# Two attention and two FFN blocks on one core: GpSimd constants ahead of the first layer-norm powers, and the second attention layer's last output chunk as seven block products

## The chip, the cores and the metric

The kernel runs on one core of one Trainium2 chip. The metric is the device time of one launch in microseconds (us); the time given is the median of three launches.

## The reference

Four residual blocks in a row, with the same weights used twice. S is 2048 tokens, D is 512, there are 32 heads of 16, the hidden width of the FFN is 1376; inputs, weights and output are bf16.

```python
def _A_ref(x, wqkv, wo):          # linear attention, 32 heads of 16
    q, k, v = ...                 # x @ wqkv
    phi = lambda t: jnp.where(t > 0, t + 1, jnp.exp(t)) + 1e-6
    pq, pk = phi(q), phi(k)
    kv = jnp.einsum("bhsd,bhse->bhde", pk, v)
    z = jnp.einsum("bhsd->bhd", pk)
    num = jnp.einsum("bhqd,bhde->bhqe", pq, kv)
    den = jnp.einsum("bhqd,bhd->bhq", pq, z)[..., None] + 1e-6
    return ... num / den ... @ wo

def _B_ref(x, w1, w2):
    return jnp.maximum(x @ w1, 0) @ w2

x = A_x
x = x + _A_ref(_layernorm(x), A_wqkv, A_wo)
x = x + _B_ref(_layernorm(x), B_w1, B_w2)
x = x + _A_ref(_layernorm(x), A_wqkv, A_wo)
x = x + _B_ref(_layernorm(x), B_w1, B_w2)
```

## The kernel before

The tokens lie in 16 tiles of 128, and four tiles make a chunk. The four blocks are layers 0 to 3: 0 and 2 are attention, 1 and 3 the FFN. The residual `xres` (128 x 512 a tile, f32) and all weights stay in SBUF.

**How the order is made.** The Python code doesn't issue instructions as it is read. Each operation is added to a graph with its engine, what it reads and writes, and a duration (the constants `C_...` in ns). A list scheduler (L383) then builds one queue for each engine: of the operations whose inputs it holds for ready it takes the one with the smallest `prio`, which is its place in the code plus an entry of the table `HINTS` (L340). An entry `"name!"` picks the engine where the code allows two. Operations of DVE and GpSimd that must not stand side by side carry a lock; names that begin with an entry of `SMALLS` (L58) have the short kind. An `odep` between two operations sets their order in a queue only; it is no wait on the chip.

**A layer norm in the first layer.** `ln_stats_first` (L772) takes BN_STATS (L773) and BN_AGGR (L774) of a tile on DVE. `ln_part_first` (L776) makes `rstd`: for the tiles named in `RSTD_ACT` by two small ScalarE instructions, Ln and Exp (L779 and L781); otherwise by a small add on DVE (`veps`, L784) and a power on GpSimd (L786). Tiles 0 to 5 are done one by one, 6 and 7 together, 8 to 11 together, 12 to 15 together. `ln_norm` (L808) then normalises with one instruction a tile into `xn` (L811), and the transposed copy `Tb` is made: for tiles 0 to 5 by TensorE and a copy out of PSUM (L847), for the others by DMA transposes that SP issues (`tr_dma`, L826). When a chunk has been transposed, `ones_col` (L1042) has GpSimd set the last column of its `xn` to 1.0, so that the products with phi(K) also give the sum z; the matmuls that read `big` (phi of K) and `xn` wait for this.

**Constants.** GpSimd fills the constants at the start (L694 to L760): the identity (L697), masks for the heads by affine selects (`m1f` L751, `bmask` L753, `hm` L757 and L760), and two memsets (L748, L749).

**Attention.** phi(K) and phi(Q) are in the unit store `big`; the sums over tokens give K/V products, which are folded with `wo` into `Mf` (128 x 4 x 512). For each chunk `a_fin_chunk` (L1182) then multiplies phi(Q) by `Mf`: four tiles with four matmuls of 512 columns each, and for each tile `resid` (L886) adds the product to the residual on DVE (L889), which also gives the row sum, and `sq` (L894) squares it on ScalarE for the row's variance. `ln_half` makes the next layer's norm for two tiles at a time. q and k products of some chunks (`a7`), the FFN's first products (`b_h7`) and its second (`b_out`) are seven block products in place of eight, with sums of blocks on DVE (for q and k, L951 and its neighbours), drains on DVE such as L1558 and a copy of one product into another PSUM bank on ScalarE (`seed`, L624). `f7` (L1207) and `f7_sums` (L1198) do the same for the output products of attention; the table `F7` (L573), which says for which layers and chunks, has none. All matmuls of these groups are issued in `mm_group` (L878, matmul L882).

**Loads.** SP issues all loads but one of `wqkv`, the DMA transposes, and the spread transfers of the attention denominators (L1155, four groups of four a layer). The first FFN weight is loaded at L726, the second at L727 and L730.

The step that picks between the two forms of the output products:

```python
def p2(t):                       # L1734, once for each chunk
    if t in F7[layer]:
        f7(t, first_layer)
    else:
        a_fin_chunk(t, first_layer)
    if t == 0 and F7[layer]:
        f7_sums()
```

## Time and profile before

| | us |
|---|---|
| median of 3 launches | 263.32 (263.13 to 263.42) |
| the profiled launch | 263.28 |
| its span in the trace | 261.5 |
| granted TensorE clock, mean | 1.0 of full speed |

"Span" is the stretch from the first to the last recorded instruction. PE is TensorE's matmuls, PEld its weight loads, DVE VectorE, ACT ScalarE, POOL GpSimd, SP the engine that issues DMAs; a letter q behind an engine is its own queue. The costliest GpSimd rows of the page's groups (line, engine, operation, output and inputs, shapes, number | busy us, mean ns of one | idle time before and what ended it):

```profile
L803 POOL TENSOR_TENSOR rstd<-veps,nhalf 128x2 f32<-128x2 f32 x24 | 17.9, 747 | 13.7 <-DVE veps L801 13.1
L816 POOL TENSOR_SCALAR xn<-xres,mean,rstd 128x512 f16<-128x512 f32 x12 | 10.1, 839 | 0.3
L795 POOL TENSOR_SCALAR mean<-s 128x2 f32<-128x2 f32 x24 | 8.6, 361 | 51.1 <-DVE xres L889 49.9
```

The first two are the power and the normalisation of the later layer norms, the third the row means. GpSimd is idle for most of the span; its idle time, like that of any engine that isn't the bound, costs nothing by itself.

### The profile page before, as it was taken

The page shows a single profiled execution, that of the slowest core. Times are in us where ns is not written, and L with a number is a line of the kernel's source. Part 1 is how long each engine was busy: PE and PEld are TensorE (multiplying, and loading weights), DVE is VectorE, ACT ScalarE, POOL GpSimd, SP SyncE. Part 2 cuts the span into 40 slices and gives each one's busy share as a digit, 9 for nine tenths or more (in the row PEclk, how much of TensorE's full clock was granted, in tenths as well). Part 3 has the DMA queues.
Part 4 walks back from the last instruction along what each step waited for, and adds up shares of the span by engine and source line. Part 5 has one row for each costly group of instructions (what it writes and reads, how often), then busy time and mean ns, then how long its engine had stood idle before and what let it go on. Part 6 is the DMA issues. An engine that isn't in the chain of part 4 may idle for free.

```text
span 261.5 us, 5847 instructions
## 1 busy us (share of the span) xinstructions
PE 255.0 (98%) x2166; PEld 199.2 (76%) x2176; DVE 231.7 (89%) x572; ACT 194.9 (75%) x426; POOL 68.9 (26%) x159
## 2 busy tenths in 40 slices
PE   7999799999999999999999999999999999999995
PEld 3654378744788888888988878774478889988884
DVE  5999979699999998899999989859988987996874
ACT  4899979769999569598999899885999746441200
POOL 1144900009834025012530440002863500000000
PEclk9999999999999999999999999999999999999999
DMA  6758860635644004400524031048351154210104
GB/s 200 282 136 150 305 213 0 153 90 120 96 64 94 10 20 83 80 4 0 101 42 43 1 59 25 3 102 192 71 106 36 36 69 120 43 40 3 80 3 160
DMA packets 46268, 22.46 MB, mean 86 GB/s; under 512 B 35904, under 2 KB 44704, under 8 KB 46240
## 3 DMA queue, kind: packets, MB, share of 16 engines
q1 hardware_dynamic: 45968, 21.83, 36.1%
q8 instruction: 17, 0.28, 0.5%
q10 hardware_dynamic: 272, 0.26, 0.4%
q14 instruction: 11, 0.09, 0.1%
HBM read 7.14 MB, written 2.10 MB: 35 GB/s over the span
## 4 chain that ended last, share of the span: by engine, by line
PE 87%; DVE 4%; issue 3%; ACT 3%; DMA 2%; POOL 1%
PE ps L882 86%; DVE bst L773 2%; DMA Tb<-xn 1%; DVE xn L811 1%; DMA xin<-in_A_x_dram 1%; POOL hm L757 1%; ACT escr L864 1%; ACT xres L864 1%; ACT big L862 1%; ACT Tb L847 0%; PE ps L841 0%; PE ps L768 0%; DVE mv L774 0%; ACT rstd L781 0%; DVE KVT L1088 0%
## 5 line engine op out<-in xcount | busy, mean ns | idle before, releaser
L882 PE MATMUL ps<-big,xn 128*128 128x256 bf16 (+1 forms) x220 | 31.8, 286 | 1.9 <-POOL xn L1043 1.7
L624 ACT ACTIVATE ps<-ps 128x512 f32<-128x512 f32 (+1 forms) x41 | 22.1, 547 | 15.3 <-PE ps L882 14.3
L882 PE MATMUL ps<-w,big 128*128 128x256 bf16 (+1 forms) x256 | 32.5, 272 | 0.0
L897 ACT ACTIVATE sqscr<-xres 128x512 bf16<-128x512 f32 x48 | 29.9, 624 | 3.3 <-DVE xres L889 2.5
L882 PE MATMUL ps<-Mf,big 128*128 128x512 bf16 x126 | 28.5, 379 | 0.1
L882 PEld LDWEIGHTS ps<-big,xn 128*128 128x128 f16 x224 | 21.2, 98 | 8.5 <-POOL xn L1043 2.0
L882 PEld LDWEIGHTS ps<-w,big 128*128 128x128 bf16 (+1 forms) x256 | 25.0, 98 | 3.0
L1354 ACT ACTIVATE big<-ps 128x512 bf16<-128x512 f32 (+1 forms) x32 | 16.1, 514 | 12.1 <-PE ps L882 11.9
L1367 DVE CUSTOM_DVE_ANT_0 big<-ps,escr 128x512 bf16<-128x512 f32 (+1 forms) x38 | 22.7, 602 | 2.4 <-PE ps L882 1.9
L882 PE MATMUL ps<-Tb,w 128*128 128x256 f16 x160 | 24.0, 273 | 0.0
L882 PE MATMUL ps<-xn,w 128*128 128x256 f16 x160 | 23.7, 272 | 0.0
L1390 ACT ACTIVATE escr<-ps 128x512 f32<-128x512 f32 (+1 forms) x38 | 19.2, 536 | 5.6 <-PE ps L882 5.6
L882 PEld LDWEIGHTS ps<-Mf,big 128*128 128x128 bf16 x128 | 12.2, 98 | 14.5 <-ACT Mf L1095 0.5
L882 PE MATMUL ps<-xn,xin 128*128 128x256 f16 x160 | 23.0, 272 | 0.0
L795 POOL TENSOR_SCALAR mean<-s 128x2 f32<-128x2 f32 x24 | 8.6, 361 | 51.1 <-DVE xres L889 49.9
L803 POOL TENSOR_TENSOR rstd<-veps,nhalf 128x2 f32<-128x2 f32 x24 | 17.9, 747 | 13.7 <-DVE veps L801 13.1
L882 PE MATMUL ps<-wqkv,Tb 128*128 128x512 bf16 (+1 forms) x94 | 19.7, 343 | 0.1
L821 ACT ACTIVATE xn<-xres,nbias,rstd 128x512 f16<-128x512 f32 x24 | 18.8, 807 | 0.5 <-DVE nbias L805 0.3
L882 PE MATMUL ps<-w,Tb 128*128 128x96 bf16 (+2 forms) x176 | 17.3, 224 | 0.0
L882 PEld LDWEIGHTS ps<-Tb,w 128*128 128x128 bf16 x160 | 15.5, 98 | 2.2 <-DVE w L1314 0.2
L882 PEld LDWEIGHTS ps<-xn,xin 128*128 128x128 bf16 x160 | 15.6, 98 | 1.9
L882 PEld LDWEIGHTS ps<-xn,w 128*128 128x128 bf16 x160 | 15.4, 98 | 1.9
(145 smaller groups left out, 624.8 us busy)
## 6 DMA issues: line engine op xcount, KB each, us to landing
big<-rdc SPq DMA_DIRECT2D x32, 128.0 KB, 2.7
w<-in_B_w_dram SPq DMA_DIRECT2D x1, 1376.0 KB, 8.3
w<-in_B_w_dram SPq DMA_DIRECT2D x1, 1280.0 KB, 11.2
xin<-in_A_x_dram SPq DMA_DIRECT2D x2, 512.0 KB, 6.7
wqkv<-in_A_wqkv_dram SPq DMA_DIRECT2D x3, 256.0 KB, 5.1
xin<-in_A_x_dram SPq DMA_DIRECT2D x4, 128.0 KB, 2.9
xin<-in_A_x_dram SPq DMA_DIRECT2D x2, 256.0 KB, 5.1
wqkv<-in_A_wqkv_dram SPq DMA_DIRECT2D x1, 512.0 KB, 4.2
```

The costliest lines, as they stand in the source:

```text
L624: g.add(ACT, lambda e: e.activation(psv[:, b, 0:w], psv[:, src, 0:w], ACTF.Identity), [("ps", src)], [("ps", b)], C_ACT_PSUM if w == 512 e ...
L757: g.add(POOL, lambda e: e.affine_select(hm1[:].rearrange("p (a b) -> p a b", b=4), ones_v, [[-16, 8], [0, 4]], ALU.is_ge, 0.0, base=0, cha ...
L773: g.add(DVE, lambda e: e.bn_stats(bst[:, i, :], xin[:, i, :]), [("xin", i)] + list(after), [("bst", i)], C_DVE_BNST, name="bnst%d" % i)
L795: g.add(POOL, lambda e: e.tensor_scalar(mean[:, sl], s1[:, sl], -INV_D, None, ALU.mult), [("s1", i) for i in tl], [("mean", i) for i in tl ...
L803: g.add(POOL, lambda e: e.tensor_tensor(rstd[:, sl], veps[:, sl], nhalf[:, 0:n], ALU.pow), [("veps", lo), ("nhalf",)], [("rstd", i) for i ...
L821: (ACT, lambda e: e.activation(xn[:, i, :], src, ACTF.Identity, scale=rstd[:, i:i + 1], bias=nbias[:, i:i + 1]), C_ACT_SB_AP)],
L864: g.add(ACT, lambda e: e.activation(sap, psv[:, b, :], ACTF.Exp), [("ps", b)], skeys, C_ACT_EXP, name=name + "_exp")]
L882: last = e.matmul(o, l, r, start=st, stop=sp, skip_group_check=skip)
L897: g.add(ACT, lambda e: e.activation(sqscr[:, q, :], xres[:, i, :], ACTF.Square, scale=math.sqrt(INV_D), accum_out=s2[:, i:i + 1]), xr(i), ...
L1354: g.add_flex([(ACT, lambda e: e.activation(ap, src(), ACTF.Relu), C_ACT_PSUM if w == 512 else 270.0), (DVE, lambda e: e.tensor_scalar(ap, ...
L1367: g.add(DVE, lambda e: e._custom_dve(dve_ops.TENSOR_ADD_SAT, out=ap, in0=sh(psv[:, bank, 0:w]), in1=sh(other()), s0=FMAX, s1=0.0), [("ps", ...
L1390: g.add(ACT, lambda e, w=w: e.activation(q[:, 0:w], psv[:, bank, 0:w], ACTF.Identity), [("ps", bank)], key, C_ACT_PSUM if len(cs) == 2 els ...
```

## The change

- **Output products.** `F7` names chunk 3 of layer 2. Its 16 matmuls of 512 columns become 28 of 256 (seven products of four matmuls) by `f7`. `f7_sums` makes four sums of blocks of `Mf` on DVE, into the store `GT`; `f7` makes four sums of blocks of phi(Q), and drains the seven products into the residual by halves of the columns. The row sums then come as two halves, which GpSimd adds.
- **Constants first.** Every first-layer power that runs on GpSimd and every ones-column memset gets an order behind all GpSimd constants (`pool_setup`).
- **rstd.** `RSTD_ACT` loses 6, 8 and 12: the rstd of tiles 6 and 7, 8 to 11 and 12 to 15 is made by the add on DVE and a power on GpSimd of 128x2, 128x4 and 128x4.
- **DVE only.** The normalisations of tiles 6 and up in the first layer and the four subtractions `wvless` may no longer be taken by GpSimd.
- **Planner.** Two durations are raised (`C_POOL_POW`, `C_POOL_SMALL`), the memset of the ones column counts 90 ns, the small adds ahead of the first-layer powers (but tiles 4 and 5) get the name `fveps`, which is in `SMALLS`. The whole table `HINTS` is new: of some 1,800 entries 1,533 have another number.

```diff
-C_POOL_POW = 690.0
+C_POOL_POW = 720.0
...
-C_POOL_SMALL = 180.0
+C_POOL_SMALL = 230.0
...
-SMALLS = ("var", "veps", "nbias")
+SMALLS = ("var", "veps", "fveps", "nbias")
...
-HINTS = {"0.aqsum1": -54, "0.aqsum2": -52, "0.aqsum3": 52, "0.aqsum4": 70, "0.as1": 46, ...
+HINTS = {"0.aqsum1": -44, "0.aqsum2": -19, "0.aqsum3": -22, "0.aqsum4": 55, "0.as1": -13, ...
...
-        F7 = {0: (), 2: ()}
+        F7 = {0: (), 2: (3,)}
...
-        RSTD_ACT = (0, 1, 2, 3, 6, 8, 12)
+        RSTD_ACT = (0, 1, 2, 3)
...
+        pool_setup = [o for o in g.ops if o.eng == POOL]
...
-                  ..., C_DVE_SMALL, name="veps%d" % lo)
+                  ..., C_DVE_SMALL, name=("veps%d" if lo in (4, 5) else "fveps%d") % lo)
             g.add(POOL, lambda e: e.tensor_tensor(rstd[:, lo:hi], veps[:, lo:hi], nhalf[:, 0:hi - lo], ALU.pow),
-                  ..., C_POOL_POW1, name="rstd%d" % lo)
+                  ..., C_POOL_POW1, name="rstd%d" % lo).odeps.extend(pool_setup)
...
-                g.add_flex([(DVE, f, C_DVE_NORM_BF)] + ([(POOL, f, C_POOL_NORM)] if i >= PE_TILES else []),
+                g.add_flex([(DVE, f, C_DVE_NORM_BF)],
...
-                g.add_flex([(DVE, f, 335.0), (POOL, f, C_POOL_ADD)], ..., name="wvless%d" % m)
+                g.add_flex([(DVE, f, 335.0)], ..., name="wvless%d" % m)
...
-                  ..., C_POOL_SMALL / 2, name="onec%d" % lo)
+                  ..., 90.0, name="onec%d" % lo).odeps.extend(pool_setup)
```

The functions that now run for layer 2's last chunk, cut to their core (`t` is 3; a11 to a22 are blocks of phi(Q), b11 to b22 of `Mf`, `tw` the sums in `GT`, `sb_` the sums of phi(Q)):

```python
def f7_sums():
    ...
    for (o, a, b, rd, k) in ((t1, b12, b11, lo, 0), (t2, b22, t1, hi + gk[0], 1),
                             (t3, b22, b12, lo + hi, 2), (t4, b21, t2, hi + gk[1], 3)):
        g.add(DVE, ... e.tensor_tensor(o, a, b, ALU.subtract), ..., name="fwsum%d" % (k + 1))

def f7(t, first_layer):
    ...                                     # four sums of phi(Q) on DVE, fsum1 to fsum4
    BA, BC = alloc_bank(), alloc_bank()
    def prod(n, bank, X, W, opens, reads):  # 4 matmuls of 256 columns
    def mid(n, bank, i0, hf):               # DVE: two tiles' half columns += bank
    def fin(n, bank, i0, hf):               # DVE: the same tile by tile, with the row sum
    prod(1, BA, a11, b11, ...)
    BB = seed(BA, 512, ...)                 # ScalarE: copy of the bank
    prod(5, BC, sb_[0], tw[0], ...)
    prod(6, BA, sb_[1], tw[1], ...)
    mid("m5", BC, f1, 1)
    prod(2, BB, a12, b21, ...)
    mid("m6", BA, f0, 1)
    fin("c11", BB, f0, 0)
    prod(7, BA, sb_[2], tw[2], ...)
    prod(3, BC, sb_[3], b22, ...)
    fin("c22", BA, f1, 1)
    fin("c12", BC, f0, 1)
    sq(f0)
    sq(f0 + 1)
    ln_half(t, 0, halves=True)
    prod(4, BA, a22, tw[3], ...)
    ...
```

What the new table and the new orders do to the queues, at the three places that the prediction speaks of. In each row: line (in the changed kernel the lines from `pool_setup` on are 2 higher), operation, output and inputs, shape, and how many stand in a row.

GpSimd's queue from the identity on, up to the ones columns (`hm`, `m1f`, `bmask` are masks, `nbexp` and `hr` constants; `MEMSET xn` sets ones columns), before:

```order
L697 AFFINE_SELECT ident<-onesf 128x128
L786 TENSOR_TENSOR rstd<-veps,nhalf 128x1
L751 AFFINE_SELECT m1f<-onesf 128x128
L786 TENSOR_TENSOR rstd<-veps,nhalf 128x1
L811 TENSOR_SCALAR xn<-xin,mv,rstd 128x512
L1043 MEMSET xn 128x4 x2
L757 AFFINE_SELECT hm<-onesf 128x32
L1043 MEMSET xn 128x4
L753 AFFINE_SELECT bmask<-m1f 128x128
L748 MEMSET nbexp 128x2
L1043 MEMSET xn 128x4
L760 AFFINE_SELECT hm<-hm 128x32
```

The same place in the changed kernel:

```order
L697 AFFINE_SELECT ident<-onesf 128x128
L751 AFFINE_SELECT m1f<-onesf 128x128
L748 MEMSET nbexp 128x2
L757 AFFINE_SELECT hm<-onesf 128x32
L749 MEMSET hr 128x1024
L753 AFFINE_SELECT bmask<-m1f 128x128
L760 AFFINE_SELECT hm<-hm 128x32
L788 TENSOR_TENSOR rstd<-veps,nhalf 128x1
L788 TENSOR_TENSOR rstd<-veps,nhalf 128x2
L788 TENSOR_TENSOR rstd<-veps,nhalf 128x1
L788 TENSOR_TENSOR rstd<-veps,nhalf 128x4 x2
L1045 MEMSET xn 128x4 x4
```

All constants now stand behind the identity and ahead of the first power, three powers are new, the normalisation has gone to DVE, and the four memsets have only powers ahead of them; before, the select of L757 stood between the second and the third memset.

DVE's queue in the first layer, from the normalisations of chunk 2 to those of chunk 3 (`bst` and `mv` are the statistics; `Mf` takes the sums of the q weights here, since its place is still free; `escr` is the exp part of phi), before:

```order
L811 TENSOR_SCALAR xn<-xin,mv,rstd 128x512 x2
L773 BN_STATS bst<-xin 128x6 x3
L774 BN_AGGR mv<-bst 128x2
L811 TENSOR_SCALAR xn<-xin,mv,rstd 128x512
L774 BN_AGGR mv<-bst 128x2 x3
L935 TENSOR_TENSOR Mf<-wqkv 128x512
L935 TENSOR_TENSOR Mf<-wqkv,Mf 128x512
L870 TENSOR_SCALAR escr<-escr 128x1024
L811 TENSOR_SCALAR xn<-xin,mv,rstd 128x512 x3
```

The same place in the changed kernel:

```order
L813 TENSOR_SCALAR xn<-xin,mv,rstd 128x512 x3
L775 BN_STATS bst<-xin 128x6
L813 TENSOR_SCALAR xn<-xin,mv,rstd 128x512
L776 BN_AGGR mv<-bst 128x2
L775 BN_STATS bst<-xin 128x6 x2
L776 BN_AGGR mv<-bst 128x2 x3
L872 TENSOR_SCALAR escr<-escr 128x1024
L786 TENSOR_SCALAR veps<-mv 128x4
L937 TENSOR_TENSOR Mf<-wqkv 128x512
L813 TENSOR_SCALAR xn<-xin,mv,rstd 128x512 x3
```

There is one normalisation more (the one that GpSimd had), the small add `veps` stands ahead of the last three, one of the two weight sums has moved behind them, and the last three wait for a power on GpSimd.

PE's queue at layer 2's output products (`Mf` with `big`: output products; `GT` with `big`: those of the seven that read a sum of `Mf`; `Tb` with `w` and `xn` with `xin`: block products of layer 3, whose sums are kept in `xn` and `xin`), before:

```order
L882 MATMUL ps<-Mf,big 128x512 x4
L882 MATMUL ps<-wo,KVT 128x512 x2
L882 MATMUL ps<-Mf,big 128x512 x60
L882 MATMUL ps<-Tb,w 128x256 x8
L882 MATMUL ps<-w,Tb 128x96 x16
L882 MATMUL ps<-xn,xin 128x256 x8
```

The same place in the changed kernel:

```order
L884 MATMUL ps<-Mf,big 128x512 x34
L884 MATMUL ps<-Mf,big 128x256 x4
L884 MATMUL ps<-Mf,big 128x512 x12
L884 MATMUL ps<-GT,big 128x256 x4
L884 MATMUL ps<-Mf,big 128x256 x4
L884 MATMUL ps<-GT,big 128x256 x4
L884 MATMUL ps<-Tb,w 128x256 x8
L884 MATMUL ps<-GT,big 128x256 x4
L884 MATMUL ps<-Tb,w 128x256 x8
L884 MATMUL ps<-w,Tb 128x96 x16
L884 MATMUL ps<-Mf,big 128x256 x4
L884 MATMUL ps<-xn,xin 128x256 x18
```

The first of the seven products stands among the other chunks' wide matmuls, the rest among the first products of layer 3; a seventh, of `GT`, follows behind the last row. On SP the load of `w` at L727 has moved from ahead of the 16 spread transfers of layer 0 to behind 12 of them, and the load of `wvl` (L721) from behind five DMA transposes to behind three.

More of the change, by code (lines that the diff above doesn't have):

```diff
@@ L1039, in wv_less_last @@
                 f = (lambda e, m=m: e.tensor_tensor(wqkv[:, m, 2 * D:3 * D], wqkv[:, m, 2 * D:3 * D], wvl[:], ALU.subtract))
-                g.add_flex([(DVE, f, 335.0), (POOL, f, C_POOL_ADD)], [("wv0",), ("wvl",)], [("wv", m)], name="wvless%d" % m)
+                g.add_flex([(DVE, f, 335.0)], [("wv0",), ("wvl",)], [("wv", m)], name="wvless%d" % m)
         def ones_col(lo, n):
             g.add(POOL, lambda e: e.memset(xn[:, lo:lo + n, D - 1:D], 1.0),
-                  [], [("xn", i) for i in range(lo, lo + n)], C_POOL_SMALL / 2, name="onec%d" % lo)
+                  [], [("xn", i) for i in range(lo, lo + n)], 90.0, name="onec%d" % lo).odeps.extend(pool_setup)
         def a_zc():
```

6 lines of the change are left out of this document (3 added, 3 removed), and 438 rows, old and new, of the table HINTS.

## The prediction

> **What bounds the kernel now.** I read the page first: the share of each engine and the granted clock.
>
> ```profile
> span 261.5 us, 5847 instructions
> PE 255.0 (98%) x2166; PEld 199.2 (76%) x2176; DVE 231.7 (89%) x572; ACT 194.9 (75%) x426; POOL 68.9 (26%) x159
> PEclk9999999999999999999999999999999999999999
> ```
>
> PE is busy for 98% of the span at full clock, so time can come only from fewer TensorE columns or from PE's idle time. Where that idle time is, the chain of work that ended last says (start, length, what):
>
> ```profile
> 6.94 0.60 ACT Tb L847
> ...
> 7.66 0.21 ACT rstd L781
> ...
> 20.16 3.04 DMA Tb<-xn
> ...
> 23.25 0.23 POOL xn L1043
> 23.48 1.99 POOL hm L757
> 25.47 6.47 issue
> 31.94 0.12 POOL xn L1043
> ...
> 32.11 5.18 PE ps L882 x39
> ...
> 183.23 75.65 PE ps L882 x693
> ```
>
> From 32.11 to 258.88 the chain is PE alone but for 0.05 us at a time and one 0.43 us DVE step. Before 32.11 it runs through GpSimd. PE's own waits, the third view, have one entry over a microsecond behind the start:
>
> ```profile
> PE ps L882 <- POOL xn L1043: 1.7, 1, 1.7
> ```
>
> GpSimd's and PE's timelines show the place (start, length, engine, line; in brackets the idle time before):
>
> ```profile
> 23.30 8.69 POOL L757 TENSOR_SCALAR_AFFINE_SELECT hm<-onesf 128x32 f32<-128x32 f32 x1
> ...
> 32.84 0.27 POOL L760 TENSOR_SCALAR_AFFINE_SELECT hm<-hm 128x32 bf16<-128x32 f32 x1
> ...
> 29.81 0.60 PE L882 MATMUL ps<-big,xn 128*128 128x256 bf16 x4
> 32.11 1.15 PE L882 MATMUL ps<-big,xn 128*128 128x512 bf16 x5 [1.71 <-POOL xn L1043]
> ```
>
> The 128x32 affine select at L757 took 8.69 us, its sister at L760 0.27. Behind it stood the memset that writes the ones column, and for that PE waited. The four matmuls from 29.81 take 4 x 0.109 us (below), so the next group could have started at 30.24 and started at 32.11: **1.87 us lost**.
>
> **The change part by part.**
>
> *GpSimd constants first.* The select and the other constants move ahead of the first rstd, to where DVE runs its statistics. Seven short instructions stand behind the identity (ends at 1.39); even at 0.95 us each, the longest unhindered one shown (the 128x1024 memset), they end at 8.0. Before, the first power started only at 9.77, so they cost nothing.
>
> ```profile
> 9.77 0.56 POOL L786 TENSOR_TENSOR rstd<-veps,nhalf 128x1 f32<-128x1 f32 x1 [8.38 <-DVE veps L784]
> 63.20 0.95 POOL L749 MEMSET hr<- 128x1024 bf16 x1
> ```
>
> Then the ones-column memsets (0.12 and 0.23 us in the chain) have only powers ahead of them and their own waits for transposes. One of them stands behind the wait for the last chunk's transposes: normalised by 23.3 (below), issued and landed some 3.04 us later, with one more transpose ahead in SP's queue, they are there by 28; PE reads that memset's column 40 wide and 8 narrow matmuls behind its group at 21.84, at 21.84 + 8.63 + 0.87 = 31.3. The stall goes: **-1.87 us**. Next late would be DVE's phi of K, which the same products read; it comes next.
>
> *Rstd by power.* Six small ScalarE instructions (0.21) go and two copies out of PSUM come to it from DVE (0.60, as L847): nothing on balance. DVE gains three small adds, GpSimd one 128x2 and two 128x4 powers. No 128x4 power is in the trace. Nearest rows:
>
> ```profile
> L803 POOL TENSOR_TENSOR rstd<-veps,nhalf x24: 688/712/1007, 59.9 to 205.8; 128x2 f32<-128x2 f32 x24
> L786 POOL TENSOR_TENSOR rstd<-veps,nhalf x2: 552/556/560, 9.8 to 12.9; 128x1 f32<-128x1 f32 x2
> ```
>
> One column more costs 0.156 us, so four columns take an estimated 0.556 + 3 x 0.156 = 1.02 us. The low end is one column's 0.556. As a high end, an 8.69 us hold like the select's needs DVE to keep issuing; here DVE has one two-input sum queued (0.42, as L951 below) and then itself waits for the power, so 1.02 + 0.42 = 1.44. I take 1.02. Behind it on DVE stand the normalisation of tiles 12 to 15, then min-adds and the first sum for chunk 2's q products (L951):
>
> ```profile
> 20.06 0.30 DVE L774 BATCH_NORM_AGGREGATE mv<-bst 128x2 f32<-128x6 f32 x3
> 21.05 0.42 DVE L870 TENSOR_SCALAR escr<-escr 128x1024 bf16<-128x1024 bf16 x1
> 21.38 1.05 DVE L811 TENSOR_SCALAR xn<-xin,mv,rstd 128x512 f16<-128x512 bf16 x3
> 24.61 0.42 DVE L951 TENSOR_TENSOR big<-Tb 128x512 f16<-128x512 f16 x1
> 35.18 0.43 DVE L872 TENSOR_TENSOR big<-big,escr 128x512 bf16<-128x512 bf16 x1 [0.99 <-ACT big L862]
> ...
> 21.84 6.41 PE L882 MATMUL ps<-wqkv,Tb 128*128 128x512 bf16 x28
> ```
>
> Ahead of the last aggregates DVE gains tile 9's normalisation and a power wait and loses two copies out of PSUM, so I keep their 20.06. Spaced as here: aggregates and min-add 0.22 + 0.33, add 0.08, power 1.02 with some 0.15 of hand-over, so tile 12's normalisation starts at 21.9 (before: 21.38). Three normalisations (1.05), three min-adds (1.0), one normalisation (0.32) and two weight sums (0.7) later, at 25.0, comes the sum, done at 25.4. PE has the same columns ahead of its group at 21.84 in both orders; in the new one 16 wide and 4 narrow matmuls follow (0.2158 and 0.109 us, below), and at 21.84 + 3.45 + 0.44 = 25.7 it needs that sum; before, it needed it some 8 us later. A slack of 0.3 us. I charge **+0.2 us** for such places (bounds 0 and 1.0, the whole delay of the two powers over one-column ones, 2 x 0.46, on PE).
>
> *Seven block products in layer 2's last chunk.* Sixteen matmuls of 512 columns become 28 of 256. PE's timeline gives the spacing:
>
> ```profile
> 178.26 13.11 PE L882 MATMUL ps<-Mf,big 128*128 128x512 bf16 x59
> 191.21 1.04 PE L882 MATMUL ps<-Tb,w 128*128 128x256 f16 x8
> 192.09 0.84 PE L882 MATMUL ps<-w,Tb 128*128 128x96 bf16 x16
> ```
>
> 60 wide ones stand in the program there (one record is missing): (191.21 - 178.26) / 60 = 0.2158 us each. Eight narrow ones: (192.09 - 191.21) / 8 = 0.110; the four at 29.81 were spaced 0.109. So 16 x 0.2158 - 28 x 0.109 = 3.45 - 3.05: **-0.40 us**. Here a rule speaks against the change. The Trainium skill (TensorE: Matmul & The Clock Gate, Back-to-back issue gap) gives a sustained spacing of 81 ns at 128 columns and 131 ns at 512, and calls 216 ns the isolated one; between them 256 columns would cost an estimated 98 ns, and the seven products 28 x 98 - 16 x 131 = +0.65 us. This trace has 216 ns over 60 matmuls in a row, so I go by the trace.
>
> The products' vector work does not count as PE time if it is covered. Prices and cover:
>
> ```profile
> L1558 DVE SCALAR_TENSOR_TENSOR xres<-ps,xres 128x256 f32<-128x256 f32 x32 | 12.5, 420 | 1.4 <-PE ps L882 1.4
> L889 DVE SCALAR_TENSOR_TENSOR xres<-ps,xres 128x512 f32<-128x512 f32 x16 | 10.5, 687 | 0.2
> ...
> 168.00:178.00 10.00, 9.95 (x100) 7.26 (x100) 5.79 (x12) 8.41 (x15) 0.00 (x0) 1.00 0.42 95
> 183.00:203.00 20.00, 19.95 (x156) 14.36 (x156) 18.39 (x53) 19.82 (x51) 12.16 (x32) 1.00 0.35 70
> 203.00:213.00 10.00, 10.00 (x103) 8.93 (x102) 9.02 (x21) 5.94 (x12) 3.65 (x5) 1.00 0.51 68
> ```
>
> (Columns: stretch, length, busy PE, PEld, DVE, ACT, POOL.) Eight 128x512 sums at L951's 0.42 are 3.4 us; draining adds eight half-width and two full-width adds for four full-width ones, 8 x 0.42 + 2 x 0.69 - 4 x 0.69 = 2.0: +5.4 us on DVE, and one PSUM copy on ACT, some 0.6. From 183 to 203 DVE is idle 1.61 us and ACT 0.18. But three of the four weight sums stand ahead of the chunk's drains, where 168 to 178 has 4.2 us idle; the order takes three relus (two of 0.69, one of 0.42) and one normalisation (0.54) off DVE; and the last chunk's squares slip to behind 203, where the two engines have 5.0 us idle. I cost it at **0**; without that cover it is the slower rival.
>
> *The rest.* On SP the load of the second weight matrix moves from ahead of four groups of spread transfers to behind the third of them:
>
> ```profile
> 45.81 14.31 SPq L1155 DMA_DIRECT2D big<-rdc  x16
> w<-in_B_w_dram SPq DMA_DIRECT2D x1, 1280.0 KB, 11.2
> L1444 DVE TENSOR_TENSOR xin<-w x2: 284/552/820, 79.1 to 84.4; 128x1280 bf16<-128x1280 bf16 x1, 96x256 bf16<-96x256 bf16 x1
> ```
>
> Issued as late as 60.1, it lands at 71.3, before its first reader at 79.1: 0. PE's other columns are the same, so a new order gains nothing where PE never waits, and can only open waits.
>
> **The sum**, against the profiled execution: it took 263.28 us (261.5 of span and 1.78 around it), 0.04 below the median of 263.32. 263.28 - 1.87 - 0.40 + 0.2 = **261.2 us**.
>
> **The rivals.** *DVE's lateness takes the stall's place.* PE runs 1.87 us earlier against DVE, which the new order loads with one more normalisation (0.31) and two power waits, about 0.5 us later from tile 12 on. If half of the gain comes back as waits for sums and phi products between 25 and 50 us, the time is 262.1 (261.6 to 262.7). For it: the slack of 0.3 us. Against: DVE had 0.99 us of idle time ahead of 35.18. Chance 0.2.
>
> *The hold moves to another GpSimd instruction* (the change doesn't do what it says). A power or memset is held as the select was and PE waits about as long: 263.28 - 0.40 = 262.9. Against: memsets at 23.25 and 31.94 passed between DVE's instructions in 0.23 us or less. The Trainium skill (SBUF — State Buffer, Who interferes with whom) has GpSimd and certain DVE instructions block one another for one whole instruction; no DVE instruction here is near 8.69 us, so the trace shows a longer hold than that rule. Chance 0.06.
>
> *Vector work becomes the bound (slower).* If nothing of the 5.4 + 0.6 us moves away, 183 to 203 takes 1.8 of it and PE waits for drains up to 4.2 us: 265.4; with the three weight sums ahead (3 x 0.42), 264.1. It decides once more than about 2.6 us cannot leave that stretch: 261.2 + 2.65 is 263.85, slower by 0.2%. Against: the moves listed above. Chance 0.08.
>
> *The skill's spacing holds:* +0.65 for -0.40, 262.25; the 60 matmuls speak against it. Chance 0.02.
>
> **How the numbers follow.** My forecast has 0.64 (260.8 to 261.6). A measurement of this kernel can tell about 0.2%, 0.53 us: faster is below 262.79, slower above 263.85. Faster takes the forecast, the skill's spacing and nearly all of the first rival: 0.85; the moved hold is "same", with the tails of its neighbours: 0.08; slower 0.07. The range runs from 260.7 (no charge for thin places, and 0.3 us of the small early waits gone) to 262.7, the far end of the first rival. The moved hold and the slower rival, 0.14 together, are left out with the thin tails.
>
> **What would show it.** In the profile after: the select ends before 9 us in under 0.5 us; PE's wait on the ones column is gone; the 128x4 powers take about 1 us; PE's list of waits has nothing over 0.3 us behind 20 us; the 28 products are spaced 0.109. I am wrong if PE's waits name DVE or ACT between 25 and 50 us or between 183 and 203, or if a GpSimd row over 2 us stands there.

## The result and the profile after

| | us |
|---|---|
| before, median of 7 launches | 263.32 (261.66 to 263.55) |
| changed, median of 7 launches | 264.29 (263.82 to 265.68) |
| ratio, 95% interval | 1.0051 (1.0031 to 1.0072) |
| the changed kernel's profiled launch / its span | 265.37 / 263.6 |

The change made the kernel about 0.5% slower; 261.2 was predicted, with a range of 260.7 to 262.7. The profiled launch of the changed kernel lies some 1 us above its median. So the changed kernel was profiled a second time (`e0_after` below), and a cause counts here when both profiles have it.

First the page of the changed kernel: span, and busy time of each engine.

```profile
span 263.6 us, 5891 instructions
PE 254.4 (96%) x2178; PEld 198.9 (75%) x2188; DVE 232.3 (88%) x586; ACT 199.6 (76%) x432; POOL 61.6 (23%) x160
```

PE is busy 0.6 us less than before (255.0) and the span is 2.1 us longer: its share fell from 98% to 96%, so it waits more. GpSimd's timeline (start, length, engine, line, operation; in brackets the idle time before) shows that the step on GpSimd did what it was to do:

```profile
1.70 0.27 POOL L757 TENSOR_SCALAR_AFFINE_SELECT hm<-onesf 128x32 f32<-128x32 f32 x1
...
16.39 1.01 POOL L788 TENSOR_TENSOR rstd<-veps,nhalf 128x4 f32<-128x4 f32 x1 [2.93 <-DVE veps L786]
...
21.36 1.11 POOL L788 TENSOR_TENSOR rstd<-veps,nhalf 128x4 f32<-128x4 f32 x1 [3.96 <-DVE veps L786]
22.43 0.15 POOL L1045 MEMSET xn<- 128x4 f16 x2
27.86 0.18 POOL L1045 MEMSET xn<- 128x4 f16 x2 [5.28 <-DMA Tb<-xn]
```

The select takes 0.27 us in place of 8.69, the powers about a microsecond. PE's list of waits (what it waited for: us in total, times, longest) has lost the wait for the ones column, 1.7 us, and has new ones:

```profile
PE ps L884 <- DVE big L1167: 2.1, 3, 0.9
PE ps L884 <- DMA Tb<-xn: 1.3, 1, 1.3
...
PE ps L843 <- DVE xn L813: 0.6, 2, 0.4
PE ps L884 <- DMA wqkv<-in_A_wqkv_dram: 0.5, 1, 0.5
```

PE's timeline shows where:

```profile
14.84 1.89 PE L884 MATMUL ps<-wqkv,Tb 128*128 128x512 bf16 x8
18.06 1.04 PE L884 MATMUL ps<-Tb,wqkv 128*128 128x512 f16 x4 [1.34 <-DMA Tb<-xn]
...
57.76 7.08 PE L884 MATMUL ps<-Mf,big 128*128 128x512 bf16 x31 [0.29 <-DVE big L1167]
65.75 3.63 PE L884 MATMUL ps<-Mf,big 128*128 128x512 bf16 x16 [0.91 <-DVE big L1167]
69.22 1.04 PE L884 MATMUL ps<-Tb,w 128*128 128x256 f16 x8
...
187.35 3.20 PE L884 MATMUL ps<-Mf,big 128*128 128x256 bf16 x16 [0.85 <-DVE big L1167]
190.39 0.60 PE L884 MATMUL ps<-GT,big 128*128 128x256 bf16 x4
```

Three places, then: the transposes of tiles 6 and 7 at 18 us, the scaled phi(Q) of layer 0's last chunks at 58 and 66 us, and the same for the first of the seven products at 187 us. The second profile, `e0_after`, has the waits at 18 and 66 us again and none in its list at 58 or 187:

```profile
PE ps L884 <- DMA Tb<-xn: 1.5, 1, 1.5
...
PE ps L884 <- DVE big L1167: 0.9, 1, 0.9
```

The span cut into stages says what each is worth (stretch, length, busy time and number of instructions of PE, PEld, DVE, ACT, POOL; clock, DMA share, GB/s). The cuts are the first block product of layer 1 (`Tb,w`) and the first output product of layer 2 (`Mf,big`). Before:

```profile
0.00:68.32 68.32, 64.70 (x418) 38.20 (x425) 60.33 (x154) 58.02 (x131) 23.26 (x42) 1.00 0.59 163
68.32:176.97 108.65, 108.49 (x1029) 94.25 (x1030) 99.61 (x261) 93.25 (x198) 28.55 (x77) 1.00 0.27 47
176.97:261.50 84.53, 81.84 (x724) 66.77 (x722) 71.71 (x159) 43.67 (x100) 17.05 (x41) 1.00 0.32 73
```

And after:

```profile
0.00:69.22 69.22, 63.87 (x419) 37.41 (x426) 59.62 (x156) 58.73 (x128) 15.13 (x40) 1.00 0.59 161
69.22:177.88 108.66, 108.50 (x1029) 94.25 (x1032) 99.48 (x260) 94.38 (x201) 29.66 (x76) 1.00 0.26 48
177.88:263.60 85.72, 82.00 (x736) 67.24 (x734) 73.19 (x171) 46.44 (x105) 16.77 (x44) 1.00 0.29 71
```

The middle stage is dense and equal to 0.01 us. Layer 0 lost 0.90 us though a stall of 1.87 us left it, and the last stage lost 1.19 though its matmuls, by their spacing, need 0.40 us less. (Its busy time is 0.16 us higher all the same, because ends are modelled and a part of each gap counts as busy: the wait of 0.85 us at 187 is a delay of 1.01 by the starts of the matmuls.)

### The profile page after: what moved, and what is told of

The parts are those of the page before. It is cut to its first block, busy times and chain, and to the rows that moved or that the text cites. A ratio compares the mean times of both kernels' runs of the same rounds, so it can differ in the third digit from the quotient of the medians.

```text
span 263.6 us, 5891 instructions
## 1 busy us (share of the span) xinstructions
PE 254.4 (96%) x2178; PEld 198.9 (75%) x2188; DVE 232.3 (88%) x586; ACT 199.6 (76%) x432; POOL 61.6 (23%) x160
## 4 chain that ended last, share of the span: by engine, by line
PE 81%; DMA 6%; DVE 6%; SPq 2%; ACT 2%; issue 1%; DVEq 0%
PE ps L884 81%; DVE xres L891 3%; DMA big<-rdc 2%; DMA xin<-in_A_x_dram 2%; DMA Tb<-xn 2%; DVE big L1167 1%; SPq L1157 1%; DVE bst L775 1%; SPq L687 1%; ACT rdc L1148 0%; ACT lnd L1146 0%; DVE xn L813 0%; SPq L692 0%; DVE xin L1316 0%; ACT GT L1078 0%
## 5 line engine op out<-in xcount | busy, mean ns | idle before, releaser
L624 ACT ACTIVATE ps<-ps 128x512 f32<-128x512 f32 (+1 forms) x42 | 23.0, 559 | 10.8 <-PE ps L884 8.4
L884 PE MATMUL ps<-Mf,big 128*128 128x512 bf16 (+1 forms) x122 | 27.2, 369 | 2.2 <-DVE big L1167 2.1
L1356 ACT ACTIVATE big<-ps 128x512 bf16<-128x512 f32 (+1 forms) x35 | 17.2, 519 | 11.2 <-PE ps L884 11.1
L805 POOL TENSOR_TENSOR rstd<-veps,nhalf 128x2 f32<-128x2 f32 x24 | 20.3, 846 | 19.6 <-DVE veps L803 18.9
L884 PE MATMUL ps<-xn,w 128*128 128x256 f16 x160 | 22.7, 273 | 0.0
L823 ACT ACTIVATE xn<-xres,nbias,rstd 128x512 f16<-128x512 f32 x27 | 21.5, 812 | 0.8 <-POOL nbias L807 0.4
L797 POOL TENSOR_SCALAR mean<-s 128x2 f32<-128x2 f32 x24 | 7.5, 314 | 57.9 <-DVE xres L891 56.9
L884 PE MATMUL ps<-Tb,wqkv 128*128 128x256 f16 (+1 forms) x96 | 15.3, 291 | 1.9 <-DMA Tb<-xn 1.3
```

The costliest lines, as they stand in the source:

```text
L624: g.add(ACT, lambda e: e.activation(psv[:, b, 0:w], psv[:, src, 0:w], ACTF.Identity), [("ps", src)], [("ps", b)], C_ACT_PSUM if w == 512 e ...
L797: g.add(POOL, lambda e: e.tensor_scalar(mean[:, sl], s1[:, sl], -INV_D, None, ALU.mult), [("s1", i) for i in tl], [("mean", i) for i in tl ...
L805: g.add(POOL, lambda e: e.tensor_tensor(rstd[:, sl], veps[:, sl], nhalf[:, 0:n], ALU.pow), [("veps", lo), ("nhalf",)], [("rstd", i) for i ...
L823: (ACT, lambda e: e.activation(xn[:, i, :], src, ACTF.Identity, scale=rstd[:, i:i + 1], bias=nbias[:, i:i + 1]), C_ACT_SB_AP)],
L884: last = e.matmul(o, l, r, start=st, stop=sp, skip_group_check=skip)
L1356: g.add_flex([(ACT, lambda e: e.activation(ap, src(), ACTF.Relu), C_ACT_PSUM if w == 512 else 270.0), (DVE, lambda e: e.tensor_scalar(ap, ...
```

## The experiments

In every batch the kernel before ran on the same chip; its medians were 263.52, 263.34, 263.26 and 263.63.

**Parts of the change alone.** `e0_after` is the changed kernel again.

> The changed kernel once more, for a second profile of it. If its waits are set by its order, PE waits at the same four places as in the first profile (near 9, 18, 65 and 187 us), and the time is 0.8 to 2 us above the kernel before. If they are chance of one launch, other places show.

Measured 264.46, ratio 1.0036 (1.0012 to 1.0059); its waits are above.

`e1_const` is the kernel before with the GpSimd constants first and nothing else. The order of PE, DVE, ACT and SP is that of before, word for word.

```diff
+        pool_setup = [o for o in g.ops if o.eng == POOL]
...
-                  ..., C_POOL_POW1, name="rstd%d" % lo)
+                  ..., C_POOL_POW1, name="rstd%d" % lo).odeps.extend(pool_setup)
...
-                  ..., C_POOL_SMALL / 2, name="onec%d" % lo)
+                  ..., C_POOL_SMALL / 2, name="onec%d" % lo).odeps.extend(pool_setup)
```

(and the changed kernel's entries of `HINTS` for the six constants)

> The kernel before with only its GpSimd constants moved ahead of the first power; PE, DVE, ScalarE and SP keep their order. Theory (the stall of 1.87 us was the select at L757 in GpSimd's queue, and nothing else): PE's wait on the ones column goes and no other takes its place, 1.9 us below the kernel before, about 261.4. Rival (DVE or the transposes are late just behind it and take the stall's place): at most half is gained, 262.4 or more, and PE's waits name DVE or a DMA between 25 and 40 us.

Measured **261.99, ratio 0.9956 (0.9937 to 0.9974)**: faster than both kernels. GpSimd's timeline and PE's, at the place of the old stall:

```profile
1.69 0.27 POOL L764 TENSOR_SCALAR_AFFINE_SELECT hm<-onesf 128x32 f32<-128x32 f32 x1
...
23.87 0.25 POOL L1052 MEMSET xn<- 128x4 f16 x2 [4.04 <-DMA Tb<-xn]
```

```profile
29.56 1.03 PE L891 MATMUL ps<-wqkv,Tb 128*128 128x512 bf16 x4
30.42 1.90 PE L891 MATMUL ps<-big,xn 128*128 128x256 bf16 x12
...
67.34 1.05 PE L891 MATMUL ps<-Tb,w 128*128 128x256 f16 x8
```

The stall is gone, and PE's list has only entries from the first 10 us. PE's order is the same in both kernels, so their instructions can be set side by side: the four products ahead of the stall start at 30.42 (before 29.81), the next at 30.86 (before 32.11). PE came there 0.61 us later and went on 1.25 earlier, so 1.86 us were gained at this place. The whole gain is less: 1.2 us by the ratio, 1.5 by the medians. Two things took from it in this launch. PE waited 1.4 us in the first 10 us (0.6 for `xn`, 0.5 for the load of `wqkv`, 0.3 for ACT), before 0.2; such early waits differ from launch to launch (the one for `xn` is 0.6 us in the first profile of the changed kernel and 0.2 in the second). And 0.22 us went again at layer 0's last output products, at 63.84 (before 64.87); the part on the scaled phi(Q) comes back to this.

The other two take the layers apart: `e2_l23` has layers 0 and 1 of before and layers 2 and 3 of the change, `e3_l01` the reverse.

```diff
 e2_l23, from before: HINTS of layers 2 and 3 from the changed kernel
-        F7 = {0: (), 2: ()}
+        F7 = {0: (), 2: (3,)}
 e3_l01, from the changed kernel: HINTS of layers 2 and 3 from before
-        F7 = {0: (), 2: (3,)}
+        F7 = {0: (), 2: ()}
```

> The kernel before with the seven block products of layer 2's last chunk and the new order of layers 2 and 3; layers 0 and 1 as before. Theory (the first of the seven products reads the last chunk's scaled phi(Q) some 2.6 us of PE work earlier than the wide ones did, and its spread transfers aren't there): PE waits 0.8 to 1.0 us for DVE's scaling near 187 us, less 0.4 us for the columns, so 0.4 to 0.6 above the kernel before, about 263.8, with the select's stall still there. Rival (that wait is carried over from layer 0's later transfers): no wait near 187, 0.4 below the kernel before, about 262.9.

> The changed kernel with the wide output products and the old order of layers 2 and 3. Theory (the new order of layer 0 loses 1.3 us at the transposed tiles 6 and 7 near 18 us and 1.2 us at the scaling of phi(Q) near 58 and 65 us, and something ahead of 10 us): with the 1.87 us of the stall gone, 0.5 to 1.2 us above the kernel before, 263.8 to 264.5. Rival (the seven products are what makes the changed kernel slow): 1.5 us or more below the kernel before, 261.8 or less.

Measured 265.62, ratio 1.0065 (1.0039 to 1.0090), and 266.77, ratio 1.0133 (1.0107 to 1.0160). Both are slower than the whole change and than I expected, so the halves don't add up: the two tables don't fit together, and PE waits in layers 1 and 2 where neither whole kernel does. The middle stage, 108.65 us before and 108.66 after, takes 110.31 and 111.92. In `e2_l23` the wait between the layers and that of the seven products are these; `e3_l01` waits for DVE's adds at 114 us (0.5) and for ACT's copies at 121, 137 and 162 (1.8 in three).

```profile
137.92 0.61 PE L892 MATMUL ps<-Tb,wqkv 128*128 128x256 f16 x4 [0.72 <-DMA Tb<-xn]
...
187.65 3.20 PE L892 MATMUL ps<-Mf,big 128*128 128x256 bf16 x16 [0.33 <-DVE big L1175]
```

As prices of the halves the two are of no use. They show two things about the places: the waits at 18 and 66 us come with the new order of layer 0 (`e3_l01` has them: 1.4 us for the transposes, 1.4 in two for the scalings), and the one at 187 with the seven products.

**The transposes at 18 us.** DVE normalises tiles 6 and 7, SP issues their transpose at 13.08, and it takes 4.93 us to land where before took some 3.2. Two theories: the power on GpSimd makes `xn` late (`e5_act6` gives the rstd of tiles 6 and 7 back to ScalarE), or something slows the transfer. The trace's DMA records have, on a queue of kind "instruction", packets of 16 KB: 17 in a launch, about 1 us each. Before, the first comes at 17.48, behind the transposes; in the changed kernel at 16.00, while they are in flight. In before and `e1_const` the first comes at the same PE instruction (199 matmuls and weight loads started), and between two of them PE starts about 250 more, so they look like the fetch of PE's code. The Trainium skill (Runtime: NRT & Kernel Launch, Instruction fetch mechanics) says that a sequencer fetches its code by a DMA queue of its own in blocks of 16 KiB, 256 instructions; the 2178 matmuls and 2188 weight loads on the profile's page of the changed kernel are 17.05 such blocks, and there are 17 packets. It calls the cost mostly hidden; whether that holds here is what the runs had to show. If it is PE's code, then dummy matmuls more or fewer at the start must move them: `e6_warm` cuts the warm-up's 8 matmuls of 512 columns into 32 of 128, `e12_fill` takes 7 of 8 from a group of 128-column fill matmuls near 5 us. None of these writes anything that is read.

```diff
 e5_act6
-        RSTD_ACT = (0, 1, 2, 3)
+        RSTD_ACT = (0, 1, 2, 3, 6)
 e6_warm
-                for k in range(WARM):
-                    last = e.matmul(psv[:, wt, :], wrm[:, 0:128], wrm[:, :], ...)
+                for k in range(4 * WARM):
+                    last = e.matmul(psv[:, wt, 0:128], wrm[:, 0:128], wrm[:, 0:128], ...)
 e12_fill
-                for k in range(8):
+                for k in range(1):
```

> The changed kernel with the rstd of tiles 6 and 7 by ScalarE again (Ln and Exp), all else in its order. Theory (the power made their transposes late, and so late that PE's code fetch, a 16 KB packet near 16.0 us on one of the 16 DMA engines, held up their last packets: 4.9 us to landing against 3.2 before): they are issued 0.4 us or more earlier, land in about 3.2 us by 16 us, PE's wait of 1.3 to 1.5 us on them near 18 us goes, and the time falls by 1 to 1.5 us below the changed kernel. Rival (PE simply comes to their reader too early in the new order): the wait shrinks by the 0.4 us of the earlier issue alone.

> The changed kernel with its eight dummy warm-up matmuls of 512 columns cut into 32 of 128: the same columns, 24 matmuls more in PE's code, so that PE's fetches of code come 24 matmuls earlier in the program. Theory (code fetch holds up the transposes of tiles 6 and 7): the first fetch moves from 16.0 to near 12 us, ahead of their transfer, they land in 3.2 us, PE's wait near 18 us falls from 1.3 to 1.5 us to under 0.3, and the time falls by 1 us or more. Rival (the transposes are slow for another reason, as the load of wv behind them): 4.9 us to landing and the wait stay.

> The changed kernel with seven of the eight dummy matmuls that fill PE at 5 us left out, and nothing else, so that PE's code is fetched seven matmuls later. Theory (the code fetch alone held up the transposes of tiles 6 and 7): the first fetch comes at 17.5 us or later, the transposes land in 3.2 us, PE's wait of 1.3 to 1.5 us on them is under 0.3, PE reaches layer 1's first products at 67.5 us or earlier (69.22 and 68.66 in the two profiles of the changed kernel), and the time is 0.8 to 1.4 us less, 263.0 to 263.7. Rival (DVE and the spread transfers set the pace up to 66 us, so an earlier PE waits there): PE reaches layer 1's first products at 68.3 us or later and the time stays at 264.3 or above.

Measured 263.74, ratio 1.0018 (0.9988 to 1.0047); 264.25, ratio 1.0024 (0.9995 to 1.0053); 263.46, ratio **0.9985** (0.9963 to 1.0007), by the ratios 0.5% less than `e0_after`. What the fetch did in these kernels (us, from the DMA records; the last column is PE's wait near 18 us):

| kernel | transpose of 6, 7 issued | first fetch | issue to landing | PE's wait |
|---|---|---|---|---|
| before | 12.37 | 17.48 | 3.19 | 0 |
| changed | 13.08 | 16.00 | 4.93 | 1.34 |
| e0_after | 12.75 | 15.67 | 4.93 | 1.5 |
| e5_act6 | 13.02 | 15.96 | 4.98 | 1.1 |
| e6_warm | 13.55 | 12.23 | 3.18 | 0 |
| e12_fill | 12.87 | 17.80 | 3.19 | 0 |

In `e1_const`, `e2_l23`, `e10_e1warm` and `e11_all` no fetch begins between issue and landing, and the landing takes 3.18 to 3.21 us; `e3_l01`, `e7_w2`, `e8_pqs` and `e9_f71` have one about 3 us behind the issue, and 4.93 to 5.04. The fetch moved both ways and the slow landing went each time; the power's removal left it. PE itself doesn't wait for its code: eight fetches fall into the middle stage of the changed kernel, in which PE is idle 0.16 us in all. The trace agrees there with the Trainium skill's "mostly hidden". But the transfer in flight is held up, and PE then waits for that, 1.1 to 1.5 us (0.4 in `e9_f71`, where PE came later). `e5_act6` missed what I expected: its `xn` came no earlier, since in DVE's queue the two normalisations stand behind other statistics. `e12_fill` did what I expected of it; in its timeline PE passes the place:

```profile
14.53 1.89 PE L884 MATMUL ps<-wqkv,Tb 128*128 128x512 bf16 x8
16.25 1.03 PE L884 MATMUL ps<-Tb,wqkv 128*128 128x512 f16 x4
...
63.90 3.63 PE L884 MATMUL ps<-Mf,big 128*128 128x512 bf16 x16 [0.73 <-DVE big L1167]
67.36 1.04 PE L884 MATMUL ps<-Tb,w 128*128 128x256 f16 x8
```

Not all of the wait was gained. With it gone, PE waited at 22 us for the next transposes, of tiles 8 and 9: 0.47 us in `e6_warm`, 0.44 in `e12_fill`, 0.35 in `e11_all`. They take 3.94 to 4.10 us in every kernel with the new order of layer 0 and 3.03 to 3.07 in the other four, wherever the fetch falls. The new order issues the load of `wvl` behind tiles 10 and 11, while both transposes are in flight; whether that is the reason was not tried.

`e6_warm` gained little although its wait at 18 us went too. In its launch the load of `wqkv` came late (1.28 us of wait at 9.35); its third fetch, at 48.10, fell on earlier spreads, and PE waited 0.8 us for `KVT` at 54.

**The scaled phi(Q) at 66 us.** DVE's timeline of the changed kernel, then of before, the last two scalings ahead of layer 0's last output products:

```profile
56.41 1.29 DVE L1167 TENSOR_TENSOR big<-big 128x1024 bf16<-128x1024 bf16 x2 [1.36 <-DMA big<-rdc]
...
63.99 1.70 DVE L1167 TENSOR_TENSOR big<-big 128x1024 bf16<-128x1024 bf16 x2
```

```profile
55.74 1.36 DVE L1165 TENSOR_TENSOR big<-big 128x1024 bf16<-128x1024 bf16 x2
57.01 0.68 DVE L889 SCALAR_TENSOR_TENSOR xres<-ps,xin 128x512 f32<-128x512 f32 x1
...
63.33 1.29 DVE L1165 TENSOR_TENSOR big<-big 128x1024 bf16<-128x1024 bf16 x2
```

Between the two pairs DVE is busy without a gap and does the same in both kernels but for two small instructions: nine adds of 0.61 and one sum of 0.74 (6.32 us before, 6.37 after). So the last pair starts 0.66 us later because the first did. The first waited for the spread issued at 53.62 and landed at 56.38. By the DMA records the spreads began 0.66 us earlier than before (45.15 for 45.81), but the third fetch fell on them at the same time (51.96, before 52.02). The twelfth landed at 56.38 in both kernels; in the changed one both scalings stand behind it. In `e6_warm`, whose third fetch missed these spreads, the pair waited for no transfer, and PE's wait near 65 us was 0.19. PE had no margin to meet the delay: sixteen wide matmuls, 3.47 us, stand between the first reader of the last scaling and the first product of layer 1. Before, that reader thus started at 68.32 - 3.47 = 64.85, and the scaling ended at 64.62; after, PE was ready at 65.75 - 0.91 = 64.84, and it ended at 65.69, 1.07 later.

The late start is 0.66 of this 1.07. The other 0.41 is in the rows above too: the last pair takes 1.70 us in place of 1.29, since its second scaling takes 1.10 in place of 0.69. It does so beside GpSimd's normalisation, which in the changed kernel starts ahead of the pair and before started when the second scaling was already under way (the changed kernel, then before):

```profile
63.87 1.28 POOL L818 TENSOR_SCALAR xn<-xres,mean,rstd 128x512 f16<-128x512 f32 x1
```

```profile
64.14 1.11 POOL L816 TENSOR_SCALAR xn<-xres,mean,rstd 128x512 f16<-128x512 f32 x1
```

Before, the memset of `hr` (L749, 63.20 to 64.15) filled GpSimd until then, and it is one of the constants that went to the front. In `before` and `e2_l23`, where it stands here, the second scaling takes 0.69 us; in the twelve kernels with the constants first it takes 1.09 to 1.10, or 0.97 in the two with the edit of `e8_pqs`. So the constants' move itself seems to cost something here, 0.22 us of PE in `e1_const`. No run moves the normalisation alone, so that it holds the scaling is argued, not shown.

Three edits, all to the changed kernel: `e7_w2` issues the load of the second FFN weight ahead of the spreads, as before (a rival: the load disturbs them); `e8_pqs` is to put the last scalings one and two adds forward in DVE's queue (in the queue that came of it only the first of them has passed an add, the second only a small sum); `e9_f71` is for the place at 187.

```diff
 e7_w2
-          "0.ld_w2a": 199
+          "0.ld_w2a": 30
 e8_pqs
-          "0.pqs3_0": 18, "0.pqs3_2": 20
+          "0.pqs3_0": 10, "0.pqs3_2": 12
 e9_f71
-          "2.f7_3_1": -191
+          "2.f7_3_1": -181
```

> The changed kernel with the load of the second FFN weight back ahead of the 16 spread transfers of layer 0, all else the same. Theory (DVE's scaling of the last chunk at 64 us is late by DVE's own queue, which the landing near 56.4 us starts; the load is not on its path): the spread transfers of the last group land in 2.7 us in place of 3.4 to 4.2, PE's wait of 0.9 us near 65 us stays, the time is that of the changed kernel within 0.3 us. Rival (the load holds up the spreads): that wait goes, 0.9 us less.

> The changed kernel with DVE's two scalings of layer 0's last chunk moved one and two residual adds ahead, all else the same. Theory (between 57 and 66 us DVE works back to back and PE waits for its order, not for a transfer): the scalings end by about 64.5 us, PE's wait of 0.9 us near 65 us goes and at most 0.3 us of it comes back as a wait for a PSUM bank, the time falls by 0.6 to 0.9 us. Rival (the last spread transfers are late): DVE waits for a DMA ahead of the scaling, and nothing is gained.

Measured 264.49, ratio 1.0042 (1.0009 to 1.0075), and 263.96, ratio 1.0012 (0.9987 to 1.0037). In `e7_w2` the last four spreads land in 2.5 to 2.7 us in place of 3.4 to 4.2, but PE's timeline has the same wait; so the load's new place costs nothing:

```profile
65.61 3.63 PE L884 MATMUL ps<-Mf,big 128*128 128x512 bf16 x16 [0.91 <-DVE big L1167]
```

In `e8_pqs` DVE and PE:

```profile
62.35 0.69 DVE L1167 TENSOR_TENSOR big<-big 128x1024 bf16<-128x1024 bf16 x1
...
63.57 0.97 DVE L1167 TENSOR_TENSOR big<-big 128x1024 bf16<-128x1024 bf16 x1
```

```profile
64.59 3.63 PE L884 MATMUL ps<-Mf,big 128*128 128x512 bf16 x16 [0.51 <-DVE big L1167]
```

The wait fell from 0.91 to 0.51, but little of that is the edit. From the start of the first pair to the end of the last scaling DVE took 9.08 us, in the changed kernel 9.29: 0.21 less, of which 0.13 is that the last scaling took 0.97 for 1.10. The rest is that DVE's first pair started 0.96 us earlier in this launch, and PE was ready only 0.76 earlier. An order in which both scalings pass an add was not run, so what DVE's queue could give back is open.

**The seven products at 187 us.** `e9_f71` moves the first product eight wide matmuls back in PE's queue.

> The changed kernel with the first of the seven products moved eight wide matmuls (1.7 us) later on PE, all else the same. Theory (the seven products ask for the last chunk's scaled phi(Q) earlier than its transfers and DVE's queue give it): PE's wait ahead of that product (0.85 and 0.98 us in two profiles, 0.2 in two others) is 0 in this one, and from layer 2's first output matmul to the end of PE it takes 81.3 to 81.6 us (81.9 to 82.9 in the profiles of the changed order so far, 81.6 before): 0.4 to 1 us less in all. Rival (the copy of the first product into the second bank, ScalarE, is now late): a wait of 0.3 us or more for ScalarE behind the product, and nothing gained.

Measured 264.58, ratio 1.0034 (1.0015 to 1.0052). The wait at 187 went and another came, for ScalarE's copy of the bank (`seed`, L624):

```profile
192.62 0.61 PE L884 MATMUL ps<-GT,big 128*128 128x256 bf16 x4
193.65 1.08 PE L884 MATMUL ps<-Tb,w 128*128 128x256 f16 x8 [0.42 <-ACT ps L624]
```

Where the first product keeps its place, PE's wait ahead of it follows a wait of DVE a few us earlier, for a spread that a scaling needs. In the first profile of the changed kernel the tenth spread of layer 2 took 3.55 us, DVE waited 0.56 us for it (up to 181.66), and PE's wait was 0.85; in `e5_act6` 0.78 and 0.98, in `e12_fill` 0.34 and 0.39. In `e0_after` and `e8_pqs` DVE had no such wait, and PE's list has none there. Behind its wait DVE works without a gap up to the scaling that the product reads.

**Together.** `e10_e1warm` is `e1_const` with the warm-up of `e6_warm`; `e11_all` the changed kernel with `e8_pqs`, `e9_f71` and `e12_fill` in one.

> The kernel before with its constants first (the fastest so far), and its eight dummy warm-up matmuls cut into 32 of 128 columns, so that PE's code is fetched 24 matmuls earlier; the order is the same. Theory (a code fetch of 16 KB during the transposes of tiles 6 and 7 holds them up): the first fetch moves from 18.1 us to 14 to 15 us, into their transfer; they land in 4.4 us or more in place of 3.2, PE waits 0.7 us or more for them near 16 us, and the time rises by 0.5 to 1.2 us. Rival (the changed kernel's transposes are slow by what stands around them in its order): they land in 3.2 us as before, and the time stays at 262.0.

> The changed kernel with three edits together: the scalings of layer 0's last chunk one and two residual adds ahead, the first of the seven products 1.7 us later, and seven of the eight dummy matmuls that fill PE at 5 us left out, so that PE's code is fetched seven matmuls later, behind the reader of the transposes of tiles 6 and 7. Theory (three places make the changed kernel slow, each for its own reason): the transposes land in 3.3 us and PE's wait of 1.3 to 1.5 us on them is under 0.3; the wait near 65 us is 0.5 or less; none near 187 us; in all 2 to 2.5 us below the changed kernel, 262.0 to 262.5, below the kernel before. Rival (a gain at one place is taken back at the next, as DVE's stretch from 57 to 66 us): 263 or more.

Measured 263.00, ratio 0.9988 (0.9969 to 1.0008), and 263.40, ratio 1.0003 (0.9987 to 1.0020). In `e10_e1warm` the first fetch came at 11.90, earlier than I expected, and did no harm (it ran until 13.01, the transposes went out at 12.64 and took 3.18 us). The third, at 48.75, hit spreads 4 to 8, and one at 177.70 spreads 7 to 11 of layer 2, which took 3.3 to 4.5 us. PE's list of waits got these:

```profile
PE ps L891 <- DVE KVT L1097: 0.7, 1, 0.7
PE ps L891 <- DVE big L1174: 0.5, 1, 0.5
```

The first of them stands at 53.37, the second at 180.68, behind a scaling for whose spread DVE had waited 1.79 us. The loss is nearly all in the last stage: the kernel reached layer 2's first output product at 176.13, `e1_const` at 176.00, and from there to PE's last start it took 82.86 us, `e1_const` 81.63. `e11_all` missed the 262.0 to 262.5 that I expected. It reached the first block product of layer 1 at 66.89, 0.45 ahead of `e1_const`, and lost that in the last stage (82.62 us), where it has the wait for ScalarE's copy that `e9_f71` has. The fastest of all remains `e1_const`.

## Why the prediction was wrong

- **The stall, -1.87:** right in its place and cause (`e1_const`: no wait there, 1.86 us gained at the place, 1.2 us in all by the ratio). In that kernel PE's order stayed; in the changed one the gain met the waits below. One price was left out: "they cost nothing" looked at the constants' new place and not at what would run in their old one, where GpSimd's normalisation now stands beside DVE's last scaling (0.69 to 1.10 us).
- **Rstd by power, 1.02 each:** right (1.01 and 1.11).
- **"I charge +0.2 us for such places": this is the step that failed first.** It worked out one thin place, DVE's first sum for chunk 2's q products, and there no wait came. The place that mattered is a transfer. The working used one landing time, 3.04 us, for all transposes; the one of tiles 6 and 7 takes 4.93 when a code fetch falls on it, and the new order had PE at its reader by then. That is 1.3 to 1.5 us. That a new order "can only open waits" was true, and was then priced for one row in place of each of the rows that PE, in its new order, comes to earlier.
- The same sum left out 57 to 66 us. DVE is without a gap there, PE's margin was 0.23 us, DVE began 0.66 us later, and its last scaling took 0.41 longer. That is 1.2 us of waits in the first profile, 0.9 in the second. Together the two places take 2.5 and 2.4 us, more than the 1.87: +0.90 in layer 0 in the first profile, +0.34 in the second.
- **Seven products:** the spacing was right. Twelve wide and four narrow matmuls from 187.35 to 190.39 are 3.04 us, and 12 x 0.2158 + 4 x 0.109 is 3.03; so -0.40 holds. The spacing of the Trainium skill (TensorE: Matmul & The Clock Gate, Back-to-back issue gap), the fourth rival, is not seen. **"I cost it at 0" for the vector work failed.** It counted DVE's total against DVE's idle time, when what counts is one input's time: the first product reads what the first of chunk 3's two scalings writes, and it stands 12 wide matmuls, 2.6 us, ahead of the end of the other chunks' wide ones. By the starts of the matmuls PE lost 1.01 us there (0.19 in the second profile); later in the queue (`e9_f71`) it waited for ScalarE. With the 0.25 us that PE lost in front of the two matmuls of `wo` and `KVT` at 178.56, and smaller gaps, the last stage to PE's last start came out at 82.72 and 81.90 us, before 81.62. In the ten profiles that have the seven products, 81.90 is the shortest.
- **The load of the second weight, 0:** right (`e7_w2`).
- **The rivals:** "DVE's lateness takes the stall's place" had the engine right for a part of the loss, but looked at 25 to 50 us, where no such wait came, and capped itself at 262.7. The slower rival was about the last stage alone. None had a late transfer in it. The text's own sign of error, PE's waits naming DVE between 183 and 203, is there.

What stays open: why a fetch of about 1 us delays a transfer by 1.7; why the tenth spread of layer 2 took 3.55 us in one launch and 2.73 in the next, on which the wait at 187 hangs; what slows the transposes of tiles 8 and 9; whether GpSimd's normalisation is what holds the last scaling; and how the loss divides between the halves, since `e2_l23` and `e3_l01` have waits of their own.

## What to carry to other kernels

When a change takes a stall away and reorders the rest, price them apart: the edit alone, in the old order, was the fastest kernel here. An instruction that is moved away also leaves a place behind: look at what will run there, and beside what. Where PE is 98% busy, each instruction that it reaches earlier has an input with its own landing time; list the inputs that arrive within a microsecond of their use, transfers first, and take the longest landing seen in the trace rather than the median. For a block product that replaces wide matmuls, ask when its first product's last input is ready, not how much idle time the vector engine has.

## What the runs showed of the hardware

- A queue of kind "instruction" brings 16 KB packets throughout the span, placed by PE's code; 7 matmuls fewer in that code moved the first from 16.00 or 15.67 to 17.80. Transfers that are in flight at that moment can land late: 4.9 us in place of 3.2 for a transpose (seven profiles with the fetch about 3 us behind the issue, none of the seven others), 3.4 to 4.6 in place of 2.6 for five spreads (before: those issued from 49.78 to 52.41, the fetch at 52.02). Not each one does: in the changed kernel the spread issued at 49.79, in flight at the fetch of 51.96, took 2.73.
- A GpSimd select of 128x32 takes 0.27 us at 1.70, ahead of DVE's first statistics, and took 8.69 us at 23.3 us, a place where DVE was busy for 8.66 of 8.70 us; the memsets around that place took 0.25 us or less in `e1_const`. What held it was not tried.
- A DVE product of two 128x1024 operands takes 0.69 us. Beside GpSimd's normalisation of 128x512 the last one of layer 0 took 0.97 to 1.10 in twelve kernels, though the one ahead of it, in ten of them also beside the normalisation, took 0.68 to 0.71.
